# Chunk-selected attention with a MetaFormer block: V loaded as fp32 and cast on chip, masks transposed by DMA, the first x on TensorE, copies spread over more engines, and a new order

## The chip, the core and the metric

The kernel runs on one core of a Trainium2 chip. The metric is the device time of one execution in microseconds. Runs of a kernel mostly agree within a few tenths of a per cent.

## What is computed

Attention over four batches, eight heads, 768 positions of 64 numbers, in which each query may look only at six of 24 chunks of 32 keys, followed by a normalised two-layer block on the joined heads. Cut to what matters:

```python
k_min, k_max = k_chunks.min(axis=3), k_chunks.max(axis=3)          # per chunk and dimension
ub = sum(max(q * k_min, q * k_max), axis=-1)                         # bound of each chunk's scores
ub = where(pos // 32 >= chunk, ub, -1e9)
top_chunks = argsort(ub)[..., -6:]
mask = (chunk_of_key in top_chunks) & causal
attn = softmax(where(mask, q @ k.T / 8, -1e9))
x = heads_joined(attn @ v)                                           # [4, 768, 512]
xn = (x - mean(x)) / sqrt(var(x) + 1e-6) * g_ln
out = x + relu(xn @ w_ch1) @ w_ch2                                   # 512 -> 2048 -> 512
```

Inputs and output are fp32.

## The kernel before

Two heads make a group `g`; there are 16 groups, four to a batch, and 768 rows are six blocks of 128, handled in two halves `r` (or `i`) of three blocks. Every step is a small function, and a hand-written string `ORDER` lists the calls, such as `smm.3.1.0` for group 3, half 1, bin 0. The loop at the end of the kernel calls them in that order and ties each instruction to the one before it on its engine, so every engine and every DMA queue works strictly in that order. There is no scheduler that moves anything.

The steps of a group, with their lines:

- `ld` (L162) loads q and k of a half group in batch 0, `ldb` (L172) loads q or k of a whole group later on; all go out from SP. `ldv` (L182) loads v from POOL's queue, which converts it to fp16 on the way. `w1` and `w2` load and convert the weights in four chunks each, from POOL's queue; a one-element copy ahead of each (L155, L159) ties it to a K bound.
- `turn` brings q and k to head dimensions on partitions: on TensorE in batch 0 (L218), by DVE's stream transpose later (L212).
- `kbound` (L262, L263) takes chunk minima and maxima, `kdiag` (L281 to L289) lays them out as a matmul operand, `qpos`, `qhi`, `qlo`, `qrel` prepare q and its positive part, in fp32 in batch 0 and as pairs of fp16 later.
- `bounds` (L297, L313) multiplies them on TensorE into `ub`. `select` (L326 to L332) finds the sixth largest per query and writes a mask `MN` of ones where a chunk is left out. `maskt` (L341) transposes it on TensorE, `mring` (L346, L347) copies it.
- The rings QA, QB, KA, KB hold, for the two heads of a group, 64 partitions of q or k and 64 partitions of mask rows. K's mask rows (`rrows`, L148, L149) hold a large negative number in the columns of their chunk, copied from a constant pattern RT, so one score matmul adds the mask to the scores. `qring` and `kcopy` fill the q and k halves.
- `smm` (L396) is the score matmul into four blocks per bin, `sexp` (L404) the exponent on ACT, `diag` (L411) the causal cut of diagonal blocks on POOL, `values` (L423) the product with v, and `norm` (L437, L438) the division into x. v's tile `va` has a column of ones beside the 64 numbers, so the row sum comes out of the same matmul.
- `pstat`, `centre` (L465), `rstd` (L476) make the normalised x. `xt` (L482) transposes it by DMA on SP. `m1` (L489) is layer 1, `relu` (L498) its activation on ACT, `m2` (L511) layer 2, `fin` (L520) scales and adds x, and SP stores the result.
- `warm`, `idle` and the `idle` argument of `bounds` (L306) are matmuls whose results nobody reads.

Buffers that pace the work: six raw tiles for q and k loads, five v tiles, four PSUM tiles for small products (`ps_t`), two of two banks for scores and layer 1 (`ps_m`), and four sets of rings.

## Time and profile before

| What | Value |
|---|---|
| runs | 283.49, 284.08, 287.08 us; median 284.08 |
| profiled execution | 284.41 us, span 282.5 us, granted TensorE clock 0.98 |
| TensorE (PE) busy | 268.8 us, 95% |
| VectorE (DVE) busy | 209.9 us, 74% |
| ScalarE (ACT) busy | 185.0 us, 65% |
| GpSimd (POOL) busy | 92.4 us, 33% |
| DMA | 32.41 MB in 136062 packets, 127072 of them under 512 B |
| SP's queue (q1) | 106640 packets, 45.0% of 16 engines |
| POOL's queue (q0) | 29248 packets, 27.5% of 16 engines |

Busy time of PE is that of pipelined matmuls with modelled ends, so neighbouring matmuls overlap in it, and the distance between starts is the cost that counts in a dense stretch. A busy share is a mean over the span; the kernel has a first part in which batch 0 is loaded and selected, a middle in which attention and the two layers of different batches are mixed, and an end of layers alone. [...]

### The profile page before, as it was taken

Reading aid. Unit: us, or ns where it says so; the run is one execution under the profiler, and the core shown is the slowest. Engines: PE = TensorE matmul, PEld = TensorE weight load, DVE = VectorE, ACT = ScalarE, POOL = GpSimd, SP = SyncE. Lnnn points to the kernel's source line nnn. Section 1 sums busy time; section 2 is a strip of 40 time slices with the busy share of each in tenths; the row PEclk is TensorE's granted clock in tenths of the full one; section 3 lists DMA queues with packets and bytes.
Section 4 is the critical chain, followed back from the end, with each engine's and each line's share of the span. In section 5 each row is a group of like instructions: output and inputs, shape, how many; then the busy total and the mean of one; then the engine's idle time right before and its main releaser. Section 6 shows DMA issues by size and latency. Waiting matters only on the chain.

```text
span 282.5 us, 6594 instructions
## 1 busy us (share of the span) xinstructions
PE 268.8 (95%) x2529; PEld 177.8 (63%) x2529; DVE 209.9 (74%) x627; ACT 185.0 (65%) x246; POOL 92.4 (33%) x162
## 2 busy tenths in 40 slices
PE   5899699999998999999999999999999999999994
PEld 2788567677655867666666766576667745555541
DVE  6889969999999979997779899969885842301112
ACT  2889969999946867867677776776968332423320
POOL 8816335453391022607462702410254000100100
PEclk9599979999999999999999999999999999999999
DMA  6999999999999764698997667663021120500202
GB/s 140 206 192 146 212 144 138 169 166 194 151 155 182 129 141 95 89 157 164 115 142 149 127 63 83 113 117 111 0 67 39 39 56 15 152 2 37 74 2 111
DMA packets 136062, 32.41 MB, mean 115 GB/s; under 512 B 127072, under 2 KB 132960, under 8 KB 136032
## 3 DMA queue, kind: packets, MB, share of 16 engines
q1 hardware_dynamic: 106640, 24.39, 45.0%
q0 software_dynamic: 29248, 7.34, 27.5%
q8 instruction: 20, 0.33, 0.5%
q10 hardware_dynamic: 144, 0.26, 0.4%
q14 instruction: 10, 0.08, 0.1%
HBM read 27.53 MB, written 6.29 MB: 120 GB/s over the span
## 4 chain that ended last, share of the span: by engine, by line
PE 82%; DVE 6%; DMA 5%; ACT 4%; issue 1%; SPq 0%; DVEq 0%; ACTq 0%
PE yp L511 28%; PE mm L489 27%; PE mm L396 12%; PE sm L423 6%; DMA raw<-in_k_dram 4%; PE ub L297 3%; ACT pt L404 2%; PE ub L313 2%; PE tr L218 2%; PE trh L341 1%; PE idle L357 1%; DMA raw<-in_q_dram 1%; PE ub L306 1%; DVE kc L262 1%; DVE kc L263 1%
## 5 line engine op out<-in xcount | busy, mean ns | idle before, releaser
L404 ACT ACTIVATE pt<-mm 128x1024 f16<-128x1024 f32 (+2 forms) x96 | 84.5, 916 | 20.4 <-PE mm L396 19.5
L511 PE MATMUL yp<-w2b,hT 128*128 128x512 f16 (+2 forms) x400 | 92.5, 370 | 0.0
L489 PE MATMUL mm<-xT,w1b 128*128 128x384 f16 x512 | 87.8, 326 | 1.3 <-ACT hT L498 1.2
L498 ACT ACTIVATE hT<-mm 128x768 f16<-128x768 f32 x64 | 51.3, 810 | 54.1 <-PE mm L489 53.7
L489 PEld LDWEIGHTS <-w1b 128*128 128x128 f16 x512 | 49.4, 98 | 34.5 <-issue 1.6
L511 PEld LDWEIGHTS <-hT 128*128 128x128 f16 x400 | 37.5, 98 | 34.1
L411 POOL TENSOR_SCALAR_AFFINE_SELECT pt<-pt 128x768 f16<-128x768 f16 x32 | 28.1, 885 | 77.4 <-ACT pt L404 77.3
L520 DVE SCALAR_TENSOR_TENSOR ot<-yp,rstd,x 128x512 f32<-128x512 f32 (+2 forms) x25 | 17.8, 716 | 44.5 <-PE yp L511 34.8
L396 PE MATMUL mm<-QA,KA 128*128 128x128 f16 (+2 forms) x224 | 34.2, 246 | 1.4 <-ACT pt L404 0.8
L396 PE MATMUL mm<-QB,KB 128*128 128x128 f16 (+2 forms) x224 | 34.2, 246 | 0.0
L476 POOL TENSOR_TENSOR rstd<-ve,mhalf 128x3 f32<-128x3 f32 x8 | 7.0, 873 | 58.0 <-DVE ve L473 57.9
L423 PE MATMUL sm<-va,pt 128*128 128x65 f16 x672 | 25.3, 193 | 0.6 <-ACT pt L404 0.3
L423 PEld LDWEIGHTS <-pt 128*128 128x128 f16 x672 | 24.0, 98 | 2.5 <-ACT pt L404 0.4
L396 PEld LDWEIGHTS <-KA 128*128 128x128 f16 x224 | 18.1, 98 | 11.2 <-issue 2.9
L453 DVE BATCH_NORM_STATS2 bst<-x 128x6 f32<-128x128 f32 x96 | 20.3, 278 | 0.0
L396 PEld LDWEIGHTS <-KB 128*128 128x128 f16 x224 | 17.9, 98 | 3.9 <-issue 0.4
L438 DVE TENSOR_TENSOR x<-sm,rden 128x384 f32<-128x384 f32 x32 | 17.8, 557 | 1.1
L465 DVE SCALAR_TENSOR_TENSOR xc<-x,mv,gall 128x512 f16<-128x512 f32 x24 | 16.8, 756 | 0.6 <-DMA xT<-xc 0.6
L281 POOL TENSOR_TENSOR kc<-kc 128x24 f32<-128x24 f32 x12 | 6.0, 502 | 31.3 <-DVE kc L263 21.7
L346 DVE COPY QA<-trh 64x640 f16<-64x640 f16 (+2 forms) x20 | 8.6, 428 | 8.3 <-PE trh L341 7.9
L218 PE MATMUL tr<-ident_f,raw 128*128 128x128 f32 x48 | 8.9, 316 | 4.2 <-DMA raw<-in_q_dram 2.2
L189 POOL DMA_DIRECT2D va<-in_v_dram x12 | 12.7, 1060 | 0.1
(85 smaller groups left out, 347.7 us busy)
## 6 DMA issues: line engine op xcount, KB each, us to landing
out_dram<-ot SPq DMA_DIRECT2D x23, 256.0 KB, 2.1
qnb<-in_q_dram SPq DMA_DIRECT2D x48, 96.0 KB, 3.2
knb<-in_k_dram SPq DMA_DIRECT2D x48, 96.0 KB, 3.3
va<-in_v_dram POOLq DMA_DIRECT2D x12, 192.0 KB, 5.4
w1b<-in_moe_w_ch_dram POOLq DMA_DIRECT2D x4, 512.0 KB, 8.2
w2b<-in_moe_w_ch_dram POOLq DMA_DIRECT2D x4, 512.0 KB, 7.1
raw<-in_k_dram SPq DMA_DIRECT2D x16, 96.0 KB, 4.3
raw<-in_q_dram SPq DMA_DIRECT2D x16, 96.0 KB, 4.2
```

What stands on the lines that cost most here:

```text
L218: nc.tensor.transpose(pst[:, t * P:(t + 1) * P], src[:, t], ident_f)
L396: nc.tensor.matmul(sc[:, hh, o:o + w * P], ks[:, t * P:(t + 1) * P], qs[:, s * P:(s + w) * P], start=True, stop=True,)
L404: nc.scalar.activation(st[g]["pt", r][:, 4 * i:4 * i + o].rearrange("p n h x -> p h n x"), st[g]["sc", r, i][:, :, 0:o * P].rearrange("p h ...
L411: nc.gpsimd.affine_select(out=dv, in_=dv, compare_op=ALU.is_ge, fill=0.0, base=0, pattern=[[0, 2 * TR], [1, P]], channel_multiplier=-1,)
L423: nc.tensor.matmul(pv[:, hh, s2, :], pt[:, where[t, s], hh, :], va[:, hh, t, 0:D + 1], start=(t == 0), stop=(t == s),)
L438: nc.vector.tensor_tensor(xh(b, r)[:, :, 2 * hp:2 * hp + 2, :].rearrange("p s h d -> p h s d"), pv[:, :, :, 0:D], rden.to_broadcast([P, 2, ...
L453: nc.vector.bn_stats(half(b, r)["st"][:, i, hp], xh(b, r)[:, i, 2 * hp:2 * hp + 2].rearrange("p h d -> p (h d)"),)
L465: nc.vector.scalar_tensor_tensor(h["xc"][:, i, :], xs, h["mv"][:, i, 0:1], gall, op0=ALU.subtract, op1=ALU.mult,)
L489: nc.tensor.matmul(hp_[:, i, 0:TR * P], w1b[:, kt, (m + i) * P:(m + i + 1) * P], h["xT"][:, kt], start=(kt == 0), stop=(kt == KT1 - 1),)
L498: nc.scalar.activation(h["hT"][:, m:m + 2], h["hp", m][:, :, 0:TR * P], ACTF.Relu, scale=HS)
L511: nc.tensor.matmul(h["yp", i][:, cs], h["hT"][:, kt, i * P:(i + 1) * P], w2b[:, kt, cs], start=(kt == 0), stop=(kt == KT2 - 1),)
L520: nc.vector.scalar_tensor_tensor(ot[:, cs], h["yp", i][:, cs], h["rstd"][:, i:i + 1], xh(b, r)[:, i].rearrange("p h d -> p (h d)")[:, cs], ...
```

## The change

- **V.** `ldv` loads v as fp32 into a tile `vr` of two buffers from SP's queue; a new `vcast` converts it into `va`, on POOL, ACT or DVE as the order says. A whole group's v is now loaded and cast head by head in later batches. The row pitch of `va` goes from 72 to 66.
- **Masks.** In groups 4 to 15 `maskt` transposes by DMA on SP into SBUF; batch 0 keeps TensorE.
- **First x.** For batch 0, half 0, `xt` transposes on TensorE, and `xe` copies the result.
- **Copies.** A suffix `@1` or `@2` in the order picks another engine for a call; `pick` chooses. In batch 0 q is first copied from PSUM to `q32` by `qcopy`, and the positive part and the rings are made from that, so that POOL can do them from SBUF. The pair (-q)+, q+ with minima and maxima becomes q, q+ with minima and differences, so `kdiag` subtracts in batch 0 too. K's mask rows are made from the identity matrix instead of the pattern RT, which is gone.
- **Other.** `relu` and `norm` can run on DVE or ACT. Three of the four `bounds` matmuls per row block in groups 4 to 15 take only the chunks up to the diagonal. Q of groups 0 and 1, first half, is loaded from ACT's queue. The one-element copies ahead of the weight loads are gone. Filler matmuls are placed anew through `busy`, between 3 and 33 ahead of a step. The whole order is rewritten.

By count of instructions: TensorE gives up 60 mask transposes, 24 fillers of 240 columns and 9 of 512, and gets 12 transposes of x and 61 short fillers. SP goes from 102 rows of DMA work to 145. POOL's queue gives up 28 v loads.

```diff
+    def vcast(g, i):
+        if i == 0:
+            st[g]["va"] = vap.tile([P, 2, NT, VW], F16, name="va", tag="va")
+            nc.gpsimd.memset(st[g]["va"][:, :, :, D:D + 1], 1.0)
+        va, t = st[g]["va"], st[g]["vr", i]
+        eng = pick(nc.gpsimd, nc.scalar, nc.vector)
+        if g >= HP:
+            copy(eng, va[:, i, :, 0:D], t)
+        else:
+            copy(eng, va[:, :, i * TR:(i + 1) * TR, 0:D], t.rearrange("p (h t) d -> p h t d", h=2))
...
+    def busy(o, n):
+        w = o.shape[1]
+        for _ in range(n):
+            nc.tensor.matmul(o, MN[0][:, 0, :], MN[0].rearrange("p s c -> p (s c)")[:, 0:w], start=True, stop=True)
...
     def rrows(i, r):
-        c = slice(r * TR * P, (r + 1) * TR * P)
-        nc.vector.tensor_copy(KA[i][64:P, c], RT[0:64, c])
-        nc.vector.tensor_copy(KB[i][0:64, c], RT[0:64, c])
+        n = S // CH // NR
+        c = slice(r * n, (r + 1) * n)
+        for t, o in ((KA[i], 64), (KB[i], 0)):
+            scaled(
+                pick(nc.vector, nc.gpsimd, nc.scalar),
+                t[o:o + 64, r * TR * P:(r + 1) * TR * P].rearrange("p (c e) -> p c e", e=CH),
+                ident_f[o:o + 64, o + c.start:o + c.stop].unsqueeze(2).to_broadcast([64, n, CH]), -NEGM,
+            )
...
     def ldv(g, i):
         b, hp = divmod(g, HP)
+        t = st[g]["vr", i] = ldp.tile([P, NT, D], F32, name="vr", tag="vr", bufs=2)
+        if g >= HP:
+            nc.sync.dma_start(t, v[b, 2 * hp + i].rearrange("(t p) d -> p t d", p=P))
+            return
...
     def maskt(g, i=None):
+        if g >= HP:
+            pm = prp.tile([P, NT - 1, P], F16, name="mT", tag="mT", bufs=1)
+            st[g]["pm"] = pm.rearrange("p s x -> p (s x)")
+            nc.sync.dma_start_transpose(pm, st[g]["mn"].rearrange("p s c -> p (s c)"))
+            return
...
     def xt(b, r, i):
+        if (b, r) == (0, 0):
+            pst = h["xp", i] = ps_t.tile([P, KT1, P], F16, name="xtr", tag="one")
+            for kt in range(KT1):
+                nc.tensor.transpose(pst[:, kt], h["xc"][:, i, kt * P:(kt + 1) * P], ident_h)
+            return
...
     def norm(g, r):
+        if other[0]:
+            for hh in range(2):
+                for s in range(TR):
+                    nc.scalar.activation(o[:, s, hh], pv[:, hh, s, 0:D], ACTF.Copy, scale=rden[:, hh, s])
+            return
...
     def bounds(g, i=None, idle=0):
                 for e, (nm, arr) in enumerate((("qh", 0), ("ql", 0), ("rh", 1), ("rl", 1))):
+                    w = NCH if e == 0 else (s + 1) * P // CH
                     nc.tensor.matmul(
-                        ub[:, s - 1].rearrange("p l h c -> p (l h c)"), st[g][nm][:, s * P:(s + 1) * P],
-                        BH[g % NB][:, arr].rearrange("p l h c -> p (l h c)"), start=(e == 0), stop=(e == 3),
+                        ub[:, s - 1, :, :, 0:w], st[g][nm][:, s * P:(s + 1) * P],
+                        BH[g % NB][:, arr, :, :, 0:w], start=(e == 0), stop=(e == 3),
                     )
```

The start of the order, before and after:

```
- ld.0.0 consts rrows.2.1 rinit.0 warm.8 ld.1.0 turn.0.qn.0 rrows.0.0 rinit.2 rrows.3.1 turn.0.kn.0 qpos.0.0
- ld.2.0 kbound.0.0 ld.3.0 turn.1.kn.0 turn.1.qn.0 kbound.1.0 qring.0.0 kdiag.0.0 rinit.1 kcopy.0.0 kdiag.1.0
+ ld.0.0 late ldv.0.0 consts ld.1.0 ldv.0.1 rinit.1 ld.2.0 warm.8 turn.0.kn.0.3 turn.0.qn.0 ld.3.0 rinit.2
+ vcast.0.0@2 rrows.3.1@2 ldb.4.kn ld.0.1 kbound.0.0 kdiag.0.0@1 rrows.0.0@2 rrows.1.1@1 rinit.0 rrows.0.1
+ rrows.3.0@1 qcopy.0.0 qpos.0.0@1 kcopy.0.0 ldv.2.0 turn.1.kn.0 turn.2.kn.0.33 turn.1.qn.0 bounds.0.0.4
```

## The prediction

> **What bounds the kernel now.** I read the page first (engines and slices), then the busy time in ten-microsecond stretches, then the chain of waits between 28 and 50 us, then single engines in order of time.
>
> ```profile
> PE 268.8 (95%) x2529; PEld 177.8 (63%) x2529; DVE 209.9 (74%) x627; ACT 185.0 (65%) x246; POOL 92.4 (33%) x162
> ...
> PEclk9599979999999999999999999999999999999999
> DMA  6999999999999764698997667663021120500202
> ```
>
> TensorE is the limit over the whole span, but two slices in the first 40 us run at a lower granted clock, and the DMA engines are full for the first 90 us. The stretches (columns: length, then busy time of PE, PEld, DVE, ACT, POOL, granted clock, DMA share, GB/s) show two regimes.
>
> ```profile
> 20.00:30.00 10.00, 9.76 (x126) 9.17 (x125) 9.38 (x40) 9.56 (x19) 5.76 (x10) 1.00 1.04 154
> 30.00:40.00 10.00, 7.52 (x67) 4.93 (x64) 8.97 (x33) 7.62 (x14) 2.99 (x7) 0.83 1.17 180
> ...
> 60.00:70.00 10.00, 9.36 (x155) 7.19 (x151) 9.69 (x37) 9.57 (x12) 4.16 (x10) 1.00 1.26 187
> ...
> 80.00:90.00 10.00, 8.82 (x55) 4.91 (x54) 9.96 (x12) 5.08 (x7) 6.13 (x12) 1.00 1.46 178
> ...
> 200.00:210.00 10.00, 10.00 (x93) 6.32 (x90) 8.93 (x30) 7.57 (x9) 5.67 (x8) 1.00 0.08 30
> ```
>
> From 100 to 270 us PE has no gap at all; there only less PE work makes the kernel shorter. From 50 to 100 us DVE is 97 to 99% busy and PE loses 2.3 us to it. Before 46 us PE is short of data. The chain there:
>
> ```profile
> 28.42 1.36 SPq L168
> 29.79 0.04 issue
> 29.83 5.59 DMA raw<-in_k_dram
> 35.42 0.14 issue
> 35.56 0.87 PE tr L218 x3
> 36.43 2.13 PE idle L357 x5
> 38.56 1.02 PE mm L396 x10
> ```
>
> A K load that SP issued late lands at 35.42, after 1.7 us of an empty PE, and then five filler matmuls and later four more (0.86 us) wait for the selection. The first layer-1 matmul (L489) starts at 45.95. Up to there PE did about 19 us of needed work: I counted each instruction before the first `m1` in the order by its spacing, such as 0.45 us for 8 score matmuls or 0.11 for a transpose of fp32. The rest, 27 us, is waiting, filler and half clock. From 45.95 to the last matmul's end (278.44) it is 232.5 us with 2.35 idle.
>
> **The sum's frame.** The profiled execution took 284.41 us for a span of 282.5; the median of three runs is 284.08, so the sum below stands 0.33 above it.
>
> **PE work, later batches.** Groups 4 to 15 lose 5 mask transposes each (L341): five start 0.27 us apart in all (61.02 to 61.29 in the PE's order), 60 x 0.055 = 3.3 us. `bounds` keeps one matmul of 96 columns per row block and narrows three to 32, 48, 64, 80, 96. The chain has 20 of 96 columns in 0.85 us, 42.7 ns each. In proportion the widths save 3 x (213 - 142) = 213 ns a group; with the 30 ns of a 65-column matmul (30 in 0.91) as floor they save 3 x (213 - 168) = 136 ns. Over 12 groups 2.6 or 1.6 us; I take 1.6, because nothing in this trace runs denser than 30 ns. Together -4.9 us, all where PE is full. The 12 transposes of the first x (12 x 0.055 = 0.7 us) come in the head, beside waits.
>
> **The masks' new way.** Each costs SP an issue: the x transposes took 1.19 to 2.25 us for four blocks, so 1.5 for five, and landed 2.3 to 7.1 us after, against 0.44 us on PE. `mring` comes several row blocks later in the new order, so I cost it at nothing; what hides it is the PE work of the group before. With that cover gone it is 3.5 us in each of 12 groups, up to 42; I keep 4 us of it for the range. `mT` has one buffer, so each also waits on SP for the copies of the mask before; behind it on SP stand the next loads, the `qring` copies and the stores.
>
> **DVE and ACT, 46 to 120 us** (first `m1` of batch 0 to that of batch 1). DVE loses 4 of 6 `max` (0.442 each, 1.8), five of seven pairs of mask copies (0.98 a pair, 5), two norms (1.1); it gains two `qhi`, one K pair and one cast (2.2, from the 0.33 to 0.49 of its copies): -5.7 of some 70 busy. ACT loses 5 `kcopy` (1.65), 5 `qhi` (0.84), one `qring` (0.97) and gains 18 norm pieces, 5 casts, 2 mask pairs. A 128x64 piece is not in the trace: 0.20 (1x1) to 0.38 (128x256) bound it; I take 0.22 by the line through 256 and 512 (0.60). Sum -13.4 + 4.0 + 2.5 + 2.8 = -4. So the 2.35 us of PE gaps should shrink; I take -1.5, bounds 0 and -2.35. The 11 `relu` on DVE (0.94 each, like the 768-element reduce) lie mostly after 180 us, where DVE falls to 10 to 30% from 230 on: nothing.
>
> **POOL.** It loses the 28 V issues (25.3 us) and gains K and Q copies, casts, `max`, mask copies. No plain copy of that length is in the trace:
>
> ```profile
> 113.60 0.90 POOL L411 TENSOR_SCALAR_AFFINE_SELECT pt<-pt 128x768 f16<-128x768 f16 x1 [3.76 <-ACT pt L404]
> ...
> 118.37 0.27 POOL L288 CAST BH<-BD 128x96 f16<-128x96 f32 x1
> ```
>
> For 768 elements that bounds it at 0.9 (same length) and 8 x 0.27 = 2.1 us (same operation). I take 0.9: the 1x1 cast already takes 0.18, so most of 0.27 is fixed. Between 46 and 120 us POOL gains 8 K halves, 3 `qhi`, 3 `max`, 4 mask halves and 5 casts, 18 to 19 us (44 at the high price), and loses about 9: from some 30 to 40 of 74, or 65.
>
> **Head.** V's 16 half loads move from POOL's queue to SP's (0.51 us per issue), and two loads of groups 4 and 6 come forward; Q of groups 0 and 1 leaves by ACT's queue. The first Q was issued at 1.83, now beside K at 0.80: -1.0 us. A V load now also waits until the cast two before it has freed one of two `vr` buffers, and the K and Q loads behind it on SP wait too; the casts come early (0.3 to 0.5 us each on whichever engine), so I cost that at nothing, inside rival one if it fails. POOL's ten V issues up to 12.9 us (7.9) and the row pattern (2.7) go; only the mask rows of K waited for them. The x transposes are the other term:
>
> ```profile
> 36.91 5.48 SPq L482 DMA_TRANSPOSE xT<-xc  x3
> ```
>
> They take SP from 36.9 to 42.4 and land up to 7.1 us on; layer 1 can't start before. On PE they are 12 x 0.055 us and three copies of about 0.6. What PE fills meanwhile is 2.13 + 0.86 = 3.0 us; I take 2 of it. The copies redone are a wash: ACT's head load stays near 38 us, DVE's falls by 4 (row copies of 5.4 us down to two pairs of 0.7). The granted clock costs 10 x 0.25 + 10 x 0.17 = 4.2 us of PE rate between 10 and 20 and between 30 and 40; the new filler, 33 short matmuls ahead of one transpose, may save any part of it, and I take none. Head -3.0; bounds -5.5 (all filler and the 2.5 us idle of 30 to 40), -4.2 more for the clock, and +12.4 (rival one).
>
> **Sum:** 284.4 - 3.3 - 1.6 - 1.5 - 3.0 = **275.0 us**, 3.2% faster. With the low ends it is 284.4 - 3.3 - 2.6 - 2.35 - 5.5 - 4.2 = 266.5, with none of head and gaps 279.5: its own range 267 to 280.
>
> **Two rules of the Trainium skill against it.** The head moves 172 GB/s with POOL's and SP's queues together, its engines over 90% busy from 4 us on. The Trainium skill (DMA: Bandwidth & Descriptors, Issuing engines are not separate DMA queues) says that all issuing queues end on the same 16 DMA engines, so another queue saves only the time to initiate. By it the move of V frees no bandwidth, and with only the 1.0 us of the earlier Q in the head the sum would be 277.0. On POOL, where the row says 0.9 us for 768 elements, the Trainium skill (GPSIMD Engine Reference, 3.1 Elementwise) gives about 2.6 cycles per element, its figure for two inputs, and so an estimate of 1.7 us at its 1.2 GHz; POOL's added work would be some 35 us instead of 19, still within the stretch, and the sum the same. No run so far shows such a copy.
>
> **Rivals.** *One, slower: SP becomes the bound of the head.* Before, the last batch-0 load (L168) is K of group 3, and 40 SP issues up to its end went out by 33.8 us, 0.84 us each, since the rings were full:
>
> ```profile
> 25.93 4.98 SPq L168 DMA_DIRECT2D raw<-in_k_dram  x2
> 30.95 2.84 SPq L168 DMA_DIRECT2D raw<-in_q_dram  x2
> ```
>
> Now 55 issues stand there. At the same pace that is 46.2 us, +12.4, and layer 1 waits for it: 284.4 + 12.4 - 4.9 - 1.5 = 290.4, 292 with a late mask or two. It decides once the first transposes of group 3's second half start after about 46 us. For it: the DMA row, full to 90 us. Against: by packets the load is even, since three of the four weight chunks (512 KB each, 0.8 us to issue and 8.2 to land) now come after it and the V packets were there before, on the other queue.
>
> *Two, no change: POOL takes DVE's place.* `diag` (L411) sits between exponent and value matmuls; if 27 later ones each queue behind half of a K pair at the high price (2.1 us) and a ninth of that delay reaches PE, it is 6 us: 284.4 - 4.9 - 3.0 + 6 = 282.5. For it: the same-operation row. Against: POOL idles 77 us before `diag` now.
>
> *Three, the head gains nothing:* PE waits for the selection anyway and filler is only renamed, 284.4 - 4.9 = 279.5. For it: the chain shows filler, not the x transposes, as the last thing before layer 1.
>
> **How the numbers follow.** Likeliest case 0.57, rival one 0.21, two 0.11, three 0.11. A measurement of this kernel tells about 2% from no change, 278.4 to 289.8. Two and three fall inside it, the likeliest case mostly below, rival one above: 0.57 / 0.22 / 0.21. The range takes in the likeliest case, two and three, and the near end of rival one: 267 to 290.
>
> **What would show it.** Right: the first layer-1 matmul at 41 to 45 us, PE busy about 263, no gap over 1 us after it, the bounds' spacing near 34 ns on average, V gone from the software queue. Wrong: SP issues of L172 past 40 us, K transposes waiting on DMA after 40, POOL above 60% between 46 and 120 with `diag` ahead of PE waits, or masks (`mT`) that score matmuls wait for.

## The result and the profile after

The changed kernel takes 297.46 us (median of four runs, 295.53 to 297.87), the kernel before 285.58 on the same chip: ratio 1.040, 95% interval 1.030 to 1.051. It is slower, where 275.0 with a range of 267 to 290 was forecast. Here and below a ratio and its interval go by those runs of a kernel that lie within 1.5% of its fastest, a median by all of them. The profiled execution took 297.35 us for a span of 295.1.

The page of the changed kernel: engines, then the slices of POOL, of the granted clock and of DMA, then the shares of the chain that ended last.

```profile
PE 273.3 (93%) x2509; PEld 183.6 (62%) x2509; DVE 209.1 (71%) x601; ACT 169.5 (57%) x259; POOL 153.3 (52%) x212
...
POOL 3759874699626956956369593299382200110000
PEclk9575895599999999999999999999999999999999
DMA  7787389999995889869797966715335211320022
...
PE 58%; POOL 18%; DMA 10%; DVE 5%; ACT 4%; issue 3%; SPq 1%; POOLq 0%; DVEq 0%; ACTq 0%
```

POOL, 33% before, is at 52% and stands in the chain. The clock row, one low slice and one middling before, is low or halved in six of the first eight slices, and DMA, full there before, has a hole at slice 5. Ten-microsecond stretches of the changed kernel (columns: stretch, length, busy PE, PEld, DVE, ACT, POOL, granted clock, DMA share, GB/s):

```profile
10.00:20.00 10.00, 9.07 (x69) 8.62 (x67) 5.25 (x16) 5.44 (x12) 7.21 (x10) 0.67 0.84 174
20.00:30.00 10.00, 10.00 (x70) 9.66 (x68) 7.16 (x28) 6.26 (x13) 8.61 (x13) 0.50 0.79 156
30.00:40.00 10.00, 8.24 (x96) 7.35 (x94) 8.11 (x32) 8.74 (x16) 7.11 (x12) 0.92 0.47 81
40.00:50.00 10.00, 3.69 (x49) 2.62 (x47) 6.89 (x22) 6.90 (x15) 7.35 (x11) 0.76 1.07 179
50.00:60.00 10.00, 10.00 (x100) 9.22 (x101) 3.57 (x13) 5.63 (x9) 5.43 (x5) 0.55 1.10 180
```

From 20 to 30 us and from 50 to 60 us PE is 10.00 of 10 busy, at half clock: five microseconds' worth of work each. From 40 to 50 it is busy for 3.69 us only. The first layer-1 matmul starts at 59.97 us, 14.0 later than before; from there to the last matmul it is 231 us against 232.5.

I add up, over stretches of one microsecond from the start to the last matmul, PE's busy time times the granted clock ("work", fillers included), the rest of the busy time ("half clock") and the time not busy ("idle"). "Head" is up to the first layer-1 matmul, to the whole microsecond.

| Kernel | first layer 1 | head: work, half clock, idle | rest: work, half clock, idle |
|---|---|---|---|
| before | 45.95 | 34.0, 4.8, 7.2 | 230.1, 0.0, 2.9 |
| after | 59.97 | 31.6, 14.7, 13.7 | 227.0, 0.0, 4.0 |

In all: 5.5 us less work, 9.9 more at half clock, 7.6 more idle, which is the 12 us. The saving that the prediction was built on is there, but after the first layer-1 matmul only 3.1 us of it, and 1.1 us of that goes into new idle time; the head lost far more. Where the head waits is seen in SP's queue (columns: start, duration, queue and line, transfer):

```profile
26.94 1.02 SPq L193 DMA_DIRECT2D vr<-in_v_dram  x2
28.06 2.37 SPq L181 DMA_DIRECT2D knb<-in_k_dram  x4
35.28 1.46 SPq L193 DMA_DIRECT2D vr<-in_v_dram  x2
36.79 2.50 SPq L181 DMA_DIRECT2D qnb<-in_q_dram  x4
39.39 1.41 SPq L193 DMA_DIRECT2D vr<-in_v_dram  x2
40.90 0.97 SPq L172 DMA_DIRECT2D raw<-in_k_dram  x2
41.92 1.02 SPq L172 DMA_DIRECT2D raw<-in_q_dram  x2
```

Between 30.4 and 35.3 us SP issues nothing, which is the hole in the DMA row. The list of waits says why, and TensorE's rows show what came late:

```profile
SPq L193 <- POOL va L201: 4.9, 1, 4.9
```

```profile
47.66 0.87 PE L233 MATMUL tr<-ident_f,raw 128*128 128x128 f32 x3 [2.75 <-DMA raw<-in_k_dram]
49.87 0.87 PE L233 MATMUL tr<-ident_f,raw 128*128 128x128 f32 x3 [1.33 <-DMA raw<-in_q_dram]
```

A V load waits for one of the two `vr` buffers (the list names the one-column fill of `va`, L201, which ends with the cast at 35.3 us), the cast that frees the buffer stands in POOL's queue, and group 3's second K and Q stand behind the V load: issued at 40.9 and 41.9 us, 25.9 and 31.0 before. What POOL did meanwhile, in its own order of time:

```profile
28.80 2.30 POOL L247 TENSOR_SCALAR r<-q 128x384 f32<-128x384 f32 x2
31.18 1.39 POOL L113 TENSOR_SCALAR QA<-q 64x384 f16<-64x384 f32 x1
32.64 1.17 POOL L113 TENSOR_SCALAR QB<-q 64x384 f16<-64x384 f32 x1
33.88 0.87 POOL L436 TENSOR_SCALAR_AFFINE_SELECT pt<-pt 128x768 f16<-128x768 f16 x1
34.75 0.51 POOL L105 CAST va<-vr 128x384 f16<-128x384 f32 x1
```

The cast takes 0.51 us; the work ahead of it takes six. So two theories: **SP**, loads in the wrong place of the queue, and **POOL**, whose maxima and multiplies are dear. The two are linked: the second would explain why SP stood. A third, **clock**, was that the gaps count mainly through the half clock that follows them.

### The profile page after: what moved, and what is told of

Its sections match the earlier page's. It is cut to its first block, busy times and chain, and to the rows that moved or that the text cites. A ratio compares the mean times of both kernels' runs of the same rounds, so it can differ in the third digit from the quotient of the medians.

```text
span 295.1 us, 6680 instructions
## 1 busy us (share of the span) xinstructions
PE 273.3 (93%) x2509; PEld 183.6 (62%) x2509; DVE 209.1 (71%) x601; ACT 169.5 (57%) x259; POOL 153.3 (52%) x212
## 4 chain that ended last, share of the span: by engine, by line
PE 58%; POOL 18%; DMA 10%; DVE 5%; ACT 4%; issue 3%; SPq 1%; POOLq 0%; DVEq 0%; ACTq 0%
PE yp L556 22%; PE mm L531 16%; PE mm L421 8%; PE sm L451 4%; DMA w2b<-in_moe_w_ch_dram 3%; DMA vr<-in_v_dram 3%; PE ub L335 3%; DMA raw<-in_q_dram 2%; POOL r L263 2%; POOL q L113 2%; PE ub L322 2%; POOL pt L436 2%; PE tr L233 2%; ACT pt L429 1%; POOL KB L113 1%
## 5 line engine op out<-in xcount | busy, mean ns | idle before, releaser
L543 ACT ACTIVATE hT<-mm 128x768 f16<-128x768 f32 x53 | 43.1, 814 | 62.7 <-PE mm L531 62.5
L421 PE MATMUL mm<-QA,KA 128*128 128x128 f16 (+2 forms) x224 | 35.4, 254 | 4.0 <-ACT pt L429 3.8
L421 PE MATMUL mm<-QB,KB 128*128 128x128 f16 (+2 forms) x224 | 35.6, 255 | 0.5 <-POOL QB L105 0.5
L541 DVE TENSOR_SCALAR hT<-mm 128x768 f16<-128x768 f32 x11 | 10.4, 954 | 25.2 <-PE mm L531 25.2
L451 PE MATMUL sm<-va,pt 128*128 128x65 f16 x672 | 27.4, 196 | 0.7 <-POOL va L105 0.5
L451 PEld LDWEIGHTS <-pt 128*128 128x128 f16 x672 | 25.8, 100 | 2.5 <-issue 0.9
L509 POOL TENSOR_TENSOR rstd<-ve,mhalf 128x3 f32<-128x3 f32 x8 | 7.8, 971 | 35.4 <-DVE ve L506 35.4
L565 DVE SCALAR_TENSOR_TENSOR ot<-yp,rstd,x 128x512 f32<-128x512 f32 (+2 forms) x25 | 17.8, 720 | 11.3 <-PE yp L556 11.2
L113 POOL TENSOR_SCALAR q<-qnT 128x768 f16<-128x768 f32 x8 | 18.1, 2257 | 0.2
L105 POOL CAST va<-vr 128x384 f16<-128x384 f32 x16 | 10.2, 641 | 14.5 <-DMA vr<-in_v_dram 14.4
L233 PE MATMUL tr<-ident_f,raw 128*128 128x128 f32 x48 | 11.0, 371 | 7.1 <-DMA raw<-in_k_dram 5.8
L305 POOL TENSOR_TENSOR kc<-kc 128x24 f32<-128x24 f32 (+1 forms) x18 | 7.2, 402 | 14.4 <-DVE kc L285 14.3
```

Of the source, the lines that this page charges most:

```text
L113: return eng.tensor_scalar(o, i, by, None, op0=ALU.mult)
L233: nc.tensor.transpose(pst[:, t * P:(t + 1) * P], src[:, t], ident_f)
L421: nc.tensor.matmul(sc[:, hh, o:o + w * P], ks[:, t * P:(t + 1) * P], qs[:, s * P:(s + w) * P], start=True, stop=True,)
L451: nc.tensor.matmul(pv[:, hh, s2, :], pt[:, where[t, s], hh, :], va[:, hh, t, 0:D + 1], start=(t == 0), stop=(t == s),)
L543: nc.scalar.activation(h["hT"][:, m:m + 2], h["hp", m][:, :, 0:TR * P], ACTF.Relu, scale=HS)
L565: nc.vector.scalar_tensor_tensor(ot[:, cs], h["yp", i][:, cs], h["rstd"][:, i:i + 1], xh(b, r)[:, i].rearrange("p h d -> p (h d)")[:, cs], ...
```

## The experiments

Edits are to the order string unless a function is shown.

**Group 3's second K and Q early (first theory).**

```diff
- ... smm.0.0.1 ld.2.1 mring.1.0 ... kcopy.2.1 ld.3.1 values.2.0.7 ...
+ ... smm.0.0.1 ld.2.1 ld.3.1 mring.1.0 ... kcopy.2.1 values.2.0.7 ...
```

> The K and Q loads of group 3's second half (ld.3.1) stand in the changed kernel behind six V loads and three other loads on SP, issue at 40.9 us and 41.9 us, and the first layer-1 matmul starts at 59.97 us (45.95 us in the kernel before). Here ld.3.1 alone is moved up, to right after ld.2.1 (issue near 27 us). Theory SP: the late loads are the main part of the 14.0 us that the head loses; the first layer-1 matmul comes 8 to 11 us earlier (49 to 52 us) and the time is 286 to 290 us against 297.5. Theory POOL (the slow multiply and maximum copies on POOL, 0.84 to 1.4 us each, set the head's pace): under 3 us gained, 294.5 or more. Theory clock (whatever leaves TensorE idle for some 2 us is followed by half clock for 4 to 13 us): the stretch of half clock from 46 to 59 us goes with the wait, and the gain is at the upper end, near 11 us; the stretch from 18 to 31 us stays.

Measured: 293.43 us (292.96 to 294.02 in four runs, where the changed kernel has 295.53 to 297.87), ratio 1.032 (1.026 to 1.038). The first layer-1 matmul comes at 52.53, 7.4 us earlier, and the half clock from 46 us on is gone. But only 4.0 us reach the end: the rest of the kernel now has 7.2 us idle instead of 4.0, and 1.7 at half clock. The longest single wait there is this, in TensorE's rows of this run:

```profile
91.52 0.21 PE L322 MATMUL ub<-BH,r 128*128 128x32 f16 x2 [2.90 <-POOL r L263]
```

and POOL's rows before it:

```profile
86.86 2.82 POOL L113 TENSOR_SCALAR q<-qnT 128x768 f16<-128x768 f32 x1
89.66 1.80 POOL L263 TENSOR_SCALAR r<-q 128x640 f16<-128x640 f16 x1
```

The next group's multiply (`qhi.7`) stands ahead of the maximum (`qrel.6`) that `bounds.6` waits for. Theory SP is nearly right for the head (49 to 52 us expected, 52.53 measured) and wrong for the end (286 to 290 us), where POOL's prices show.

**POOL's multiplies and maxima of the head on DVE.**

```diff
- rrows.1.1@1 rrows.3.0@1 qpos.0.0@1 qpos.1.0@1 qring.3.0 qpos.3.0@1 rrows.1.0@1 qpos.1.1@1 qpos.0.1@1 qring.0.1 qpos.3.1@1 qring.3.1
+ rrows.1.1 rrows.3.0 qpos.0.0 qpos.1.0 qring.3.0@2 qpos.3.0 rrows.1.0 qpos.1.1 qpos.0.1 qring.0.1@2 qpos.3.1 qring.3.1@2
```

> Up to the first layer-1 matmul, the copies that the changed kernel gives to POOL as multiplies and maxima (rrows of groups 1 and 3, qpos, qring of groups 0 and 3) go to DVE; the V casts, the diagonal masks and kdiag stay on POOL, the order of loads stays. Theory POOL: selection is released earlier (first score matmul 23.65 us in the changed kernel, 17.39 us before), the first layer-1 matmul comes 6 to 10 us earlier, 287 to 292 us. Theory SP: the V casts on POOL come earlier too, so the wait of SP for a vr buffer (4.9 us, SP idle from 30.4 to 35.3 us) shrinks, and the loads behind it come 3 to 5 us earlier, but no more: 292 to 295 us. Theory clock: nothing from the copies themselves, only what the changed gaps do to the clock; if the stretch at half clock from 18 to 31 us stays, under 3 us.

Measured: 291.99 us, ratio 1.017 (1.007 to 1.027), from two runs of 288.80 and 289.65 us; that is in the range of theory POOL. Its profile is of an execution of 294.40 us, with the first layer-1 matmul at 53.29. No load was moved, yet group 3's second K is issued at 33.86 us instead of 40.90: SP stood because of POOL.

**Fillers in the waits.**

```diff
- turn.1.kn.0 ... turn.3.kn.1 ... turn.3.qn.1
+ turn.1.kn.0.50 ... turn.3.kn.1.75 ... turn.3.qn.1.40
```

> Only filler matmuls (128 columns, 0.055 us each at full clock) are added ahead of three transposes that wait for loads: 50 ahead of group 1's first K (TensorE idle from 5.7 to 8.7 us), 75 and 40 ahead of group 3's second K and Q (idle from 42 to 50 us). No load and no copy moves. Theory clock: the granted clock stays at 1.0 over 8 to 14 us and over 46 to 59 us; the dense stretch from 50 to 60 us takes half of its time, and the first layer-1 matmul comes 4 to 6 us earlier: 291 to 293 us. Theory SP and theory POOL: the loads and copies come when they came, the half clock is a symptom that something else covers, and the time stays within 1.5 us of 297.5. If the fillers outlast the waits the kernel gets slower by up to 2 us.

Measured: 299.69 us, ratio 1.048 (1.038 to 1.059). The clock is held at 8 to 14 and at 46 to 59 us as intended, head time at half clock falls from 14.7 to 6.8, and nothing is gained: the first layer-1 matmul is at 61.23. That doesn't make the half clock free. TensorE's rows in this run:

```profile
44.99 4.35 PE L221 MATMUL tr<-MN 128*128 128x128 f16 x75
49.17 0.50 PE L233 MATMUL tr<-ident_f,raw 128*128 128x128 f32 x3
53.47 0.52 PE L233 MATMUL tr<-ident_f,raw 128*128 128x128 f32 x3 [1.57 <-DMA raw<-in_q_dram]
61.23 1.46 PE L531 MATMUL mm<-xT,w1b 128*128 128x384 f16 x8
```

The 75 fillers hold K's transposes back by 1.5 us (47.66 in the changed kernel), and group 3's second Q came 3.6 us later (49.87 there). From Q's transposes to the first layer-1 matmul it is 7.76 us here at full clock, though TensorE waits for 1.6 of them, against 10.10 in the changed kernel, which runs this stretch without a wait and nearly all of it at half clock. There half clock cost 2.3 us. The run doesn't tell what theory clock would be worth without the two delays.

**All three edits.** The three diffs above together.

> The three edits together: the K and Q loads of group 3's second half right after those of group 2, the multiplies and maxima of the head on DVE instead of POOL, and the fillers. If the three causes add up, the head's 14.0 us are nearly all given back: first layer-1 matmul at 45 to 49 us and 283 to 287 us, within 2% of the kernel before. If one cause alone bounds the head, this is no better than that cause's run by more than 2 us. A remainder over 288 us would mean that something else in the head (the other load order, the V loads' own issue time on SP) costs as much again.

Measured: 293.50 us, ratio 1.032 (1.026 to 1.038). The first layer-1 matmul is at 57.94, later than with the loads alone. This run doesn't test the sum of the causes: with the loads early there is no wait left for the fillers to fill. The 75 and the 40 stand ahead of transposes that had run at 44.45 us without a wait in the run with the loads alone, and here run at 49.11 and 51.68, so the fillers themselves cost some 6.4 us (4.2 and 2.2). The ninth run has the loads early and POOL's multiplies off without any filler.

**V by the software queue.** `ldv` from POOL's queue straight into `va`, `vcast` empty:

```diff
-        t = st[g]["vr", i] = ldp.tile([P, NT, D], F32, name="vr", tag="vr", bufs=2)
-            nc.sync.dma_start(t, v[b, 2 * hp + i].rearrange("(t p) d -> p t d", p=P))
+            nc.gpsimd.dma_start(va[:, i, :, 0:D], v[b, 2 * hp + i].rearrange("(t p) d -> p t d", p=P))
```

> The changed kernel with one part undone: V goes by the software queue straight into fp16 va, issued by POOL at the same places of the order, and there is no vr and no cast. SP loses 24 issues of some 1 us (V of the first batch is 16 of them) and its wait for a vr buffer. Theory SP (group 3's second K and Q come late because SP stands behind V): they issue near 30 us instead of 40.9 us, the first layer-1 matmul comes at 50 to 53 us as it did when those two loads were moved up (52.53 us), and the time is 291 to 294 us. Theory POOL: POOL gains the issues and loses the casts of 0.5 us, its copies stay where they were, the first selection stays late (first score matmul near 23 us), and whatever SP gains is partly lost: 294 to 298 us. Theory clock: the stretch of half clock from about 17 to 31 us stays, since POOL's copies ahead of the first bounds stay.

Measured: 299.49 us, ratio 1.057 (1.050 to 1.064). Group 3's K is issued at 29.3 us, as theory SP had it, and the head is 4.8 us shorter (55.18), yet the kernel is not faster: the rest has 7.5 us idle, 4.0 of it one wait for `w2b`, whose issue is POOL's. Taking V off SP is no remedy while POOL is loaded.

**All of POOL's multiplies and maxima on DVE.** As the second run, and over the whole order:

```diff
- qhi.7@1 ... qrel.5@1 ... rrows.2.1@1
+ qhi.7@2 ... qrel.5 ... rrows.2.1
```

> As the run that moved the head's multiplies and maxima from POOL to DVE, and the same for the later batches: every qhi that POOL made (2.26 to 2.82 us each) goes to DVE (0.73 us there), every qrel maximum (1.8 us) and the late rrows too. POOL keeps the V casts, K copies, diagonal masks, kdiag. Theory POOL: the waits of TensorE on the maximum (2.26 us at 91 us in the run with the head alone off POOL) go, with the half clock behind them, and the time is 286 to 289 us (292.0 with the head alone). Rival, DVE takes the bound: DVE goes from 209 us to some 225 us busy, the maxima wait there instead, no gain: 291 to 294 us.

Measured: 290.09 us, ratio 1.024 (1.017 to 1.030), between the two expectations. First layer-1 matmul at 49.42, 10.6 us earlier than in the changed kernel, and no load was moved. Group 3's second K goes out early all the same:

```profile
34.22 0.96 SPq L172 DMA_DIRECT2D raw<-in_k_dram  x2
```

SP's wait for POOL is down from 4.9 us to 0.6. The interval overlaps that of the run with the head alone off POOL, so what the later batches add isn't shown. The 2.26 us wait on the maximum is gone; a wait of 3.4 us on `BH` took its place.

**The two TensorE cuts in the kernel before.** The changed `bounds` and `maskt`, nothing else:

```diff
+                    w = NCH if e == 0 else (s + 1) * P // CH
+                        ub[:, s - 1, :, :, 0:w], st[g][nm][:, s * P:(s + 1) * P],
...
+            nc.sync.dma_start_transpose(pm, st[g]["mn"].rearrange("p s c -> p (s c)"))
```

> The kernel before with two parts of the change alone: the narrowed bounds of the later batches and the masks of the later batches transposed by DMA into one SBUF buffer. The prediction's sum gave 1.6 and 3.3 us for these: if both reach the end, 280 to 281.5 us against 285.8. If TensorE's saved time only turns into waits (its gaps after 50 us were 2.35 us in all), or the mask's way by SP makes the score matmuls wait, 284 to 289 us.

Measured: 301.22 us, ratio 1.058 (1.049 to 1.067). This was the largest miss of an expectation. SP's queue of this kernel, and DVE's rows of the same stretch:

```profile
55.58 4.99 SPq L177 DMA_DIRECT2D qnb<-in_q_dram  x4
60.68 5.58 SPq L177 DMA_DIRECT2D knb<-in_k_dram  x4
66.36 4.23 SPq L343 DMA_TRANSPOSE mT<-MN  x1
70.71 0.52 SPq L246 DMA_DIRECT2D QA<-q  x1
```

```profile
61.49 0.93 DVE L333 TENSOR_TENSOR MN<-ubm,m 128x240 f16<-128x240 f32 x1
...
72.28 0.32 DVE L352 COPY QA<-mT 64x640 f16<-64x640 f16 x1 [8.42 <-DMA mT<-MN]
```

The mask is ready at 62.4 us; SP reaches its transpose at 66.4, behind eight loads, and DVE stands still for 8.42 us with everything else that it has to do. TensorE then waits for the QA row that SP issues after the mask:

```profile
PE mm L402 <- DMA QA<-q: 5.8, 1, 5.8
```

The rest of this kernel has 16.0 us idle and 5.9 at half clock, against 2.9 and 0.0.

**Group 3's loads early in the kernel before.**

```diff
- smm.1.0.1 ldb.4.qn ... w1.0.2 ld.3.1 smm.2.0.1
+ smm.1.0.1 ld.3.1 ldb.4.qn ... w1.0.2 smm.2.0.1
```

> The kernel before with ld.3.1 (group 3's second K and Q) moved up on SP, ahead of group 4's Q and K, which take eight issues. In the kernel before, TensorE waits 1.67 us for this K at 35.56 us, is idle from 33.8 us, and runs at half clock from 35.2 to 38.5 us. Theory SP: the same load ends the head's wait there too; it lands some 6 us earlier, the gap and the half clock go, and the first layer-1 matmul comes 3 to 5 us earlier than 45.95 us: 281 to 283 us. Rival: the next load or POOL's weight loads (w1) end the wait at nearly the same time, or group 4 comes late later on: 285 us or more.

Measured: 285.25 us, ratio 1.006 (1.001 to 1.010), the same. The first layer-1 matmul came 1.1 us earlier only (44.85): the wait for K is gone, and short waits for selections and for `xt` stand there. The rival was right.

**Loads early and all of POOL's multiplies off.** The first and the sixth together.

> The two edits that helped, together and without fillers: group 3's second K and Q moved up on SP, and all multiplies and maxima of POOL on DVE. Counted over the trace, the changed kernel has 5.5 us less TensorE work at full clock than the kernel before (258.6 against 264.1), 9.9 us more lost to half clock (14.7 against 4.8) and 7.6 us more idle (17.7 against 10.1). If the late loads and POOL's prices are separate causes, the first layer-1 matmul (49.4 us with POOL alone, 52.5 us with the loads alone) comes at 46 to 48 us and the time is 286 to 288 us. If both only feed the same gap, it is the run with POOL alone again, 289 to 291 us.

Measured: 289.16 us, ratio 1.020 (1.017 to 1.024); first layer-1 matmul at 49.69. The second expectation came: both feed the same gap. With POOL relieved the casts come in time, and the loads' place costs no more.

**The same with six fillers ahead of three bounds.**

```diff
- bounds.1.0 ... bounds.2.0 ... bounds.3.0
+ bounds.1.0.6 ... bounds.2.0.6 ... bounds.3.0.6
```

> The run before this in the list, plus the six fillers of 240 columns (0.10 us each at full clock, 1.8 us in all) ahead of the bounds of groups 1, 2 and 3 that the kernel before has and the changed kernel dropped. Theory clock: fp32 bounds matmuls of 24 columns keep TensorE busy by the profile but don't hold its clock up, the dense fillers do; the stretch of half clock near 19 to 30 us goes or shortens to under 6 us, the head gains 2 to 4 us after paying for the fillers, and the time is 2 to 4 us under its sister's. Rival: the clock drops after the gaps of 2 us and no filler behind them matters; the fillers cost 1 to 2 us, as they did in the two runs that filled waits.

Measured: 290.26 us, ratio 1.025 (1.020 to 1.030). Stretches without the fillers, then with them:

```profile
20.00:30.00 10.00, 7.77 (x77) 7.19 (x77) 9.45 (x31) 7.49 (x15) 2.46 (x5) 0.83 0.87 178
30.00:40.00 10.00, 8.28 (x92) 7.58 (x92) 7.91 (x34) 7.91 (x17) 6.50 (x12) 0.66 0.86 151
```

```profile
20.00:30.00 10.00, 7.86 (x94) 6.98 (x93) 9.17 (x30) 7.52 (x15) 2.54 (x6) 1.00 0.87 179
30.00:40.00 10.00, 6.47 (x95) 5.60 (x95) 8.62 (x36) 8.65 (x19) 5.24 (x10) 1.00 0.80 141
```

The clock is full in both stretches, and from 30 to 40 us PE is busy 6.47 us instead of 8.28 for nearly the same steps: it does them faster and then waits. First layer-1 matmul at 49.64 against 49.69. So in this head, which waits for other engines, the half clock has no price. How the fillers keep the clock up isn't shown: the last of the 18 ends at 22.6 us, and the clock is full at 33 to 39 us too, where the sister runs at half. But it isn't one execution alone: in three of four runs the mean granted clock is 0.985 to 0.988, against 0.953 to 0.962 in the sister's four.

**Masks of the later batches back on TensorE** in the ninth run's order:

```diff
-            nc.sync.dma_start_transpose(pm, st[g]["mn"].rearrange("p s c -> p (s c)"))
+        pool, tag = (ps_m, "mm") if g >= HP else (ps_t, "one")
+        pm = st[g]["pm"] = pool.tile([P, S], F16, name="trh", tag=tag)
```

The four mask copies that POOL made go to DVE.

> The first run of this list, with the masks of the later batches transposed on TensorE again (60 transposes, 0.055 us each, into a buffer of the score pool) and copied by DVE and ACT. In the kernel before, narrowed bounds and DMA masks together cost 16 us, with SP standing at a mask for DVE's selection and TensorE 5.8 us at a QA row behind it. If the masks by DMA cost that here too, TensorE's waits shrink and this is 3 us or more faster than its sister. If the changed order covers them, as the prediction had it, this is 2 to 5 us slower: 3.3 us of TensorE work comes back, and the score pool's buffers are held longer.

Measured: 311.61 us, ratio 1.098 (1.093 to 1.104). TensorE waits 11.3 us, 13 times, for exponents to free the score pool, so this run tells of that buffer and not of the masks; it is inconclusive for its question.

**Narrow bounds in the kernel before**, with group 3's loads early: the two diffs above for `bounds` and `ld.3.1`, no masks by DMA.

> The kernel before with the narrowed bounds and with group 3's second K and Q moved up, no masks by DMA. The prediction's term for the bounds is 1.6 us; moving the loads alone left the kernel the same (ratio 1.0055). If the 16 us of the run with both TensorE cuts came from the masks alone, this is 282 to 285 us, at most 1% under the kernel before. If the narrow bounds were the trouble, it is over 290 us.

Measured: 283.49 us, ratio 0.9985 (0.996 to 1.002), the same as before. Against its sister without the narrowing (1.0055) it is 0.7%, 2.0 us, with intervals that just touch. So the narrow bounds do no harm, and since the moved loads alone changed nothing either, what is left for the loss of the run with both cuts is the masks on that order's SP queue, as its rows say. It is the fastest kernel measured here, but not distinguishably faster than the kernel before.

**What is left of the head.** Three runs more, on top of the ninth: V by the software queue (its diff above); two loads of the next batch late; both with the bounds fillers.

```diff
- smm.3.0.0 ldb.6.kn sexp.1.0.1 ... maskt.0.1 ldb.5.qn diag.3.0 ... ldv.2.1 turn.3.qn.1
+ smm.3.0.0 sexp.1.0.1 ... maskt.0.1 diag.3.0 ... ldv.2.1 ldb.6.kn ldb.5.qn turn.3.qn.1
```

> The run with both edits (289.2 us, first layer-1 matmul 49.69 us against 45.95 us before), and V by the software queue straight into fp16 va again, which POOL, now at two tenths in the head, issues. In that run SP issues without a pause from 0.8 to 37.5 us, and TensorE waits at 37 us for a V that SP issued at 32 us. Theory SP: the queue is the rest of the head's loss; 16 issues of 0.5 us less put every load behind them up to 8 us earlier, the first layer-1 matmul comes at 46 to 48 us and the time is 285 to 288 us. Rival, ACT and DVE: their chain of exponentials, selection and copies (DVE idle under 5 us from 9 to 50 us) is the rest; the head stays at 49 to 50 us, 288 to 290 us. Rival, POOL: the issues of some 1 us each stand ahead of diagonal masks and K copies, 290 us or more.

> The run with both edits (289.2 us), and on SP two loads of the next batch (ldb.6.kn and ldb.5.qn, eight issues, 5.3 us of SP) moved behind the first batch's last V loads. Theory SP: the V that TensorE waits for at 37 us comes 2 to 4 us earlier, the first layer-1 matmul 1 to 2 us earlier (48 us), 287 to 288.5 us. Rival, ACT and DVE bound the head: no change, 288.5 to 290 us. If the next batch then comes late, its bounds wait after 50 us and the time is over 290 us.

> All of it: group 3's loads early, POOL's multiplies on DVE, V by the software queue, the two loads of the next batch late, and the bounds fillers that held the clock in the head (lost to half clock there 1.5 us instead of 6.3). If SP and then the clock bound the head one after the other, the head reaches the kernel before, 45 to 47 us, and with 4 us less TensorE work behind it the time is 281 to 285 us. If ACT and DVE bound it, 287 to 290 us, as its sisters.

Measured: 290.21 us, ratio 1.020 (1.010 to 1.029); 290.90, 1.023 (1.015 to 1.031); 289.17, 1.015 (1.005 to 1.025). First layer-1 matmuls at 51.66, 51.47 and 50.95. None is told apart from the ninth run by its interval; all three expectations of theory SP missed. With POOL relieved, V's queue makes no difference that these runs show.

**V and the next batch out of the start.** Three more on the ninth: V later; then also `ldb.4.kn` behind `ld.1.1` and its `turn` ahead of `kbound.4`; then also the bounds fillers.

```diff
- ld.0.0 late ldv.0.0 consts ld.1.0 ldv.0.1 rinit.1 ... vcast.0.0@2 ... ldv.2.0 ... vcast.0.1@1 ... select.1.0
+ ld.0.0 late consts ld.1.0 rinit.1 ... ld.0.1 ldv.0.0 ldv.0.1 ... select.1.0 vcast.0.0@2 ldv.2.0 vcast.0.1@1
```

> The run with both edits (289.2 us, first layer-1 matmul 49.69 us), and the first three V loads, which the changed kernel puts on SP ahead of group 1's K, with their casts behind group 3's and group 0's K and Q: SP goes back to K and Q first, as in the kernel before. There TensorE waits 1.9 us for group 1's K at 8.2 us (1.8 us too where V came by the software queue, so it is the transfer and not only the issue), and the first score matmul is at 19.1 us against 17.4 us before. Theory: V ahead of K is the rest of the head's loss; the wait at 8.2 us goes, the first score matmul comes at 17 to 18 us, the first layer-1 matmul 1.5 to 3 us earlier (47 to 48 us), 286 to 288 us. Rival, ACT and DVE in the stretch from 30 to 50 us bound it whatever comes in first: 288.5 to 290 us.

> The run ahead of it in the list, and the next batch's first load (ldb.4.kn, four issues on SP, 2.2 us) and its transpose on DVE (0.97 us) behind the first batch's second halves. Theory: each thing of a later stage that stands ahead in the head costs; 1 to 2 us less than its sister, first layer-1 matmul 46 to 47.5 us, 285 to 287 us. Rival, ACT and DVE after 30 us: the same as its sister within 1 us.

> The run ahead of it in the list, and the bounds fillers that held the clock (half clock in the head 1.5 us instead of 6.3 us, with no gain while the head waited for something else). If the waits are gone, TensorE's pace counts again and the fillers bring 1 to 3 us: 283 to 286 us, within 1% of the kernel before. If not, 287 to 290 us.

Measured: 289.71 us, ratio 1.013 (1.007 to 1.019); 290.20, 1.014 (1.008 to 1.020); 292.01, 1.021 (1.014 to 1.027). The first score matmul does come at 17.86 in the first of them, as expected, but the cast that I placed behind it stood 5.2 us on ACT for its V load and gave the lead back (first layer-1 matmul 52.87; 50.92 and 53.93 in the other two). So the start isn't cleared of the rest of the loss, and by their intervals the three are not told apart from the ninth run.

| Kernel | first layer 1 | head: work, half clock, idle | rest: work, half clock, idle |
|---|---|---|---|
| loads early | 52.53 | 34.2, 6.7, 12.1 | 226.1, 1.7, 7.2 |
| POOL relieved, all | 49.42 | 32.4, 6.4, 10.2 | 226.8, 2.5, 5.7 |
| both | 49.69 | 33.5, 6.3, 10.3 | 225.5, 2.7, 4.9 |
| both, with bounds fillers | 49.64 | 35.4, 1.5, 13.1 | 226.6, 1.4, 7.0 |
| both, V by software | 51.66 | 34.3, 5.9, 11.8 | 227.0, 0.0, 6.0 |
| before, both TensorE cuts | 44.27 | 35.8, 1.7, 6.5 | 226.2, 5.9, 16.0 |
| before, narrow, loads early | 46.09 | 35.6, 1.7, 8.7 | 228.3, 0.0, 1.7 |

**What stays open.** Of the 14 us that the head loses, moving two loads gives back 7.4 and relieving POOL 10.6, and both together 10.3. The last 3.5 us or more are there in every mended kernel, and it wasn't shown whether they come from what the new order puts first or from the copies now on DVE and ACT. In the list of waits of the run with both edits, TensorE's waits in the head have passed from loads (3.9 us before, 1.9 there) to DVE and ACT (0.7 and 6.7, without the wait at the very start). That points to the copies, but a list of waits names what came last and not what would have come next. In the rest, the mended kernel (both edits) has 4.6 us less work than before and spends it on idle time (+2.0) and half clock (+2.7); its longest wait is this, with POOL's row that began it:

```profile
68.30 0.27 PE L322 MATMUL ub<-BH,q 128*128 128x96 f16 x2 [3.28 <-POOL BH L313]
```

```profile
65.58 0.76 POOL L305 TENSOR_TENSOR kc<-kc 128x24 f32<-128x24 f32 x1 [16.06 <-DVE kc L285]
```

POOL had been idle for 16 us; it waits for DVE's chunk maxima, and the four small steps behind them (to 68.25 us) are all on TensorE's path. No run took this wait away alone.

## Why the prediction was wrong

- **TensorE's work, -4.9: right in size.** The count gives 5.5 us less, fillers included, but only 3.1 after the first layer-1 matmul, where the forecast had put all of it. The bounds' spacing is 34.5 ns on average (20 in 0.69 us; 34 forecast), and the bounds alone gave about 2.0 us in the kernel before, with intervals that just touch (1.6 forecast). But work off a full engine only shows at the end if the others keep up. With the gaps, the part behind the head was to lose 6.4 us and lost 1.4; in the run with both edits it has 4.6 us less work and is no shorter.
- **Head, -3.0: the step that failed; it measured +14.0.** Three sentences of it were wrong. "I cost that at nothing" of the `vr` wait: the casts did not come early, they came behind POOL's copies, and SP stood for 4.9 us with K and Q behind it. "The copies redone are a wash" looked at ACT and DVE only: POOL is busy 31.6 of the first 46 us instead of 23.4, with multiplies ahead of the casts and of the maxima that TensorE waits for. Taking POOL's multiplies and maxima off, with no load moved, brought the first layer-1 matmul forward by 10.6 us, moving the two loads by 7.4, both by 10.3; the last 3.5 us or more stay open. And the "33 short matmuls" were said to save any part of the clock's 4.2 us or none; the head lost 9.9 us more to half clock. A price is seen for one stretch of it, 2.3 us behind Q's late transposes, and none in the run that held the clock with both edits made.
- **The price on POOL: 0.9 us for 768 elements, the low end, for every copy.** These groups of the changed kernel (mean of one behind the busy time) show two prices:

```profile
L113 POOL TENSOR_SCALAR q<-qnT 128x768 f16<-128x768 f32 x8 | 18.1, 2257 | 0.2
L263 POOL TENSOR_SCALAR r<-q 128x640 f16<-128x640 f16 x7 | 12.7, 1819 | 0.1
...
L105 POOL CAST KA<-knT 64x768 f16<-64x768 f32 x9 | 7.5, 837 | 0.0
...
L113 POOL TENSOR_SCALAR KA<-ident_f 64x384 f16<-64x384 f32 x4 | 4.7, 1176 | 0.3
```

  Plain casts of 768 elements cost 0.84 us, near the 0.9 taken; multiplies of 768 cost 2.26, over the high end of 2.1, and maxima of 640 cost 1.82, where the same rate gives 1.75. The diff shows which is which (`tensor_copy` against `tensor_scalar`), and I priced both by one row. The estimate of 1.7 us from the 2.6 cycles per element of the Trainium skill (GPSIMD Engine Reference, 3.1 Elementwise) lies between the two measured prices. POOL from 46 to 120 us is busy 49.3 of 74 us, between the 40 and the 65 of the two prices and over the 60% that was named as the sign. The first 14 of these us are still head in the changed kernel; in the stage that was meant, from the first layer-1 matmul of batch 0 to that of batch 1 (60.0 to 133.4 us), it is 51.9 of 73.4.
- **PE gaps, -1.5: wrong in sign.** Idle time in the rest went from 2.9 to 4.0 us, though DVE's busy time fell about as forecast (in the same stage 64.3 of 73.4 us, 70.8 of 74.2 before). 1.7 us of the 4.0 is a wait for a chunk of w2, and most of what is left is POOL: it took DVE's place, as rival two said, but ahead of `bounds` (1.2 us) and of score matmuls (0.5), not at `diag`.
- **Masks by DMA at nothing: right in the new order, not in the old one.** Each is issued in 1.2 us and lands after 2.7 (1.5 and 2.3 to 7.1 forecast); TensorE waits 0.5 us for them in all. The same masks in the old order are what cost the run with both cuts some 16 us: the cover that I named, later row blocks, has to be arranged on SP's queue. The "cover gone" price of 3.5 us for each of 12 groups is not what happened there: one mask held up SP, DVE and then TensorE (5.8 us), and half clock and other waits followed.
- **Rival one, 290.4 to 292: half right.** Its signs came, SP's L172 past 40 us and K transposes waiting after 40, and its +12.4 us for the head is near the 14.0. But the pace of 0.84 us an issue did not come: 57 issues are out by 42.9 us, 4.9 of which SP stood, 0.67 us each without that. SP was late because it stood for a buffer that POOL freed, and because two loads were placed behind that. That the rings were full was read from the slow issues; no view shows how full a ring is. V off SP, with POOL relieved, changed nothing that can be told apart. It stayed under the 297.5 because it still counted the whole 6.4 us behind the head.

## What to carry to other kernels

When work moves to an idle engine, price it by operation and not only by size, and ask what it is queued ahead of: two loads and a maximum behind the wrong neighbours cost the head more than the 5 us that were truly saved on the busiest engine. A buffer count on a strictly ordered queue is a wait of everything behind it, so cost it from when the freeing instruction runs, not from how long it takes. An edit that is nearly free in one written order (0.5 us of TensorE's waits) can cost some 16 us in another. And a filler test only tells of the clock if the fillers end before the data comes.

## What the runs showed of the hardware

- A multiply or maximum on POOL takes 2.8 to 3.1 us per 1000 elements along the free dimension at 384 to 768 elements (2.26 us for 768, 1.82 for 640, 1.18 for 384), with 64 partitions as with 128 (1.18 and 1.17 for 384). A plain cast takes 0.84 for 768 and 0.50 to 0.64 for 384.
- The granted clock stayed at half from 18 to 31 us in the changed kernel with PE without a gap by its busy time. The Trainium skill (TensorE: Matmul & The Clock Gate, Part 1: The HAM clock gate) has the full clock back after one busy window of about 3.4 us; here 13 us of fp32 transposes, small bounds matmuls and score matmuls didn't bring it. With 18 dense fillers more, 1.8 us in all, the kernel with both edits ran at full clock from 12 us on, where its sister fell to half twice (22 to 26 and 32 to 40 us).
- What half clock costs depends on what comes next: 4.8 us less of it in that head moved the first layer-1 matmul by 0.05 us, while the stretch from Q's transposes on took 10.10 us in the changed kernel, nearly all at half clock and without a wait, and 7.76 at full clock in the run with fillers in the waits.
